# Gathering the preparation, row and routing pieces of a fused attention and expert kernel at one place per turn

## The chip, the cores and the metric

The kernel runs on one core of one Trainium2 chip. The metric is the device time of one execution in microseconds; the kernel before took 904.12 us (median of three runs, 903.97 to 904.96). The engines are called PE (TensorE, matmuls), PEld (its weight loads), DVE (VectorE), ACT (ScalarE), POOL (GpSimd) and SP (SyncE, which issues most DMAs). Each engine works through its own queue of instructions in order and waits on semaphores where it needs another engine's result.

## The reference

Two blocks follow each other. The first is a routed attention: for each of 4 batches and 8 heads, 768 queries and 768 keys of 64 values are each assigned to the nearest of 16 centroids, and a query attends only to keys of its own cluster. The second is a mixture of experts over the 3072 resulting rows of 512 values: a cosine router picks one of 8 experts for each row.

```python
q_assign = np.argmax(np.einsum('bhsd,hcd->bhsc', q_n, c_n), axis=-1)
k_assign = np.argmax(np.einsum('bhsd,hcd->bhsc', k_n, c_n), axis=-1)
mask = q_assign[:, :, :, None] == k_assign[:, :, None, :]
scores = np.where(mask, scale * np.matmul(q, k.transpose(0, 1, 3, 2)), -1e9)
attn = softmax(scores)                       # with 1e-9 added to the sum
x = rows of np.matmul(attn, v)               # (4*768, 8*64)
logits = xn @ en.T / tau                     # both rows normalized
expert_idx = np.argmax(logits, axis=1)
out[mask] = gate_w[mask, None] * (np.maximum(x[mask] @ w1[e], 0.0) @ w2[e])
```

## The kernel before

**Pairs, units and turns.** The attention works on pairs of heads: 16 pairs `n`, four for each batch. A pair has 12 units (two halves `hq` of the queries, six blocks `j` of 128 keys). For a unit, `scores` (L330) multiplies the block of keys with 384 queries of both heads into two PSUM banks, first with the one-hot cluster codes `kH`, `qH` (bf16) and then with `kT`, `qT` (fp32); `expo` (L346) takes the exponential on ACT into `prob`; `attend` (L351) multiplies `prob` with the values into `o_ps` and lets DVE add `prob` into `acc`. Six units make a group `g` (one half of the queries). After a group, `total` (L380) sums `acc` over the partitions on PE, ACT copies the sum as `den`, and `divide` (L395) takes a reciprocal on DVE and writes `xT`. Later `rows` (L412) transposes `xT` on PE, and ACT copies the rows into `xr`.

**Preparation of a pair.** `prep_pieces` (L209) returns ten pieces. `turn` transposes q or k, one half of the sequence at a time, three 128x128 transposes into one bank; ACT copies q, DVE copies k. `products` multiplies the transposed q and k with the centroids and ACT copies the result `asT`. `assign` transposes it back; DVE takes the maximum `amax` and compares (`sel`), POOL multiplies `sel` with a preference (L258). `choose` lets DVE take the maximum `pm` of that product and write the one-hot code `oh`. `turn_hot` transposes the code, six bf16 transposes into one bank for q (copied by DVE, L283) and for k (copied by ACT, L285). `values` adds up the values on POOL, and `mean` sums them on PE with a bank of its own (L298), from which DVE copies `ev`.

**Routing of a batch.** `route_pieces` (L429) returns five pieces: `products` of a half of the rows with the expert embeddings, `logits` with the squared norms of that half (three ACT instructions of 512 elements), the same for the other half, and `choose`, a chain of small operations on DVE, ACT (a square root and an exponential, each with its table) and POOL, which ends in a DMA of the rows to DRAM (`x_rows`).

**Banks.** All pieces, and `total`, take their PSUM bank from `misc()`: two banks in turn. `scores` has two buffers of two banks, `o_ps` two banks.

**Order.** The order on PE, DVE and ACT is that of the program (`manual_schedule`, L515); the order on SP and POOL is a planner's. The loop (L524) takes two units a turn, so a pair has six turns. One turn issues `scores` and `expo` of the two units after next, then one piece of preparation, then `rows` of the group before in the turns with `part == 4`, then `attend` of its two units, then `total` and `divide` where a group has just ended, then a second piece of preparation and one of routing. The pieces of pair `n+1` are worked through during pair `n`, one after the other, beginning with its first turn. `load` (L120) gets q, k and v of pair `n+1` at the beginning of pair `n`, through SP, each into two buffers; at pair 1 the first experts' weights follow.

After the last unit the loop runs on for three turns (`total`, `divide` and `rows` of the last group), and then come the five routing pieces of the last batch. After that a block of small operations finds each row's place (from L567), and the experts' stage (from L665) works through 28 blocks of 128 rows.

Of the kernel before, what the change touches and what calls it, by code (L numbers as in the profile page):

```python
# [9 lines left out]
F32 = mybir.dt.float32  # L10
BF16 = mybir.dt.bfloat16
I32 = mybir.dt.int32
ALU = mybir.AluOpType
ACTF = mybir.ActivationFunctionType
# [4 lines left out]
P = 128  # L19
# [16 lines left out]
def kernel(  # L36
# [12 lines left out]
    nc = tc.nc  # L49

    B, H, S, D = q.shape
# [4 lines left out]
    NJ = S // P  # L56
# [47 lines left out]
    with ExitStack() as at:  # L104
# [9 lines left out]
        def misc():  # L114
            return psM.tile([P, 512], F32, tag="misc", name="misc")
# [1 line left out]
        pairs = [(b, hp) for b in range(B) for hp in range(NHP)]  # L117
        ld = {}

        def load(n):  # L120
            b, hp = pairs[n]
            t = ld[n] = {}
            for nm, src in (("q", q), ("k", k), ("v", v)):
                t[nm] = ldp.tile([P, NJ, 2, D], F32, tag=nm + "32", name=nm + "32")
                for h in range(2):
                    nc.sync.dma_start(
                        out=t[nm][:, :, h],
                        in_=src[b, 2 * hp + h].rearrange("(p j) d -> p j d", j=NJ),
                    )

        c_sb = smp.tile([P, D], F32, name="c_sb", bufs=1)
        emb = smp.tile([E, DM], F32, name="emb", bufs=1)
        tau = smp.tile([E, 1], F32, name="tau", bufs=1)
        load(0)
        nc.scalar.dma_start(out=c_sb, in_=centroids.rearrange("h c d -> (h c) d"))
        nc.scalar.dma_start(out=emb, in_=moe_expert_emb)
        nc.scalar.dma_start(out=tau, in_=moe_tau.to_broadcast([E, 1]))
# [71 lines left out]
        def prep_pieces(n):  # L209
# [21 lines left out]
            def products():  # L231

                bk = misc()
                for i in range(4):
                    nc.tensor.matmul(  # L235
                        bk[2 * C * i : 2 * C * i + 2 * C, 0:HS],
                        lhsT=cnB[:, hp],
                        rhs=t["qk"[i // 2] + "T"][:, HS * (i % 2) : HS * (i % 2) + HS],
                        start=True,
                        stop=True,  # L240
                    )
                t["asT"] = smp.tile([P, HS], F32, tag="asT", name="asT")
                nc.scalar.copy(t["asT"], bk[:, 0:HS])

            def assign():
                bk = misc()
                for u in range(NJ // 2):
                    nc.tensor.transpose(  # L248
                        bk[:, P * u : P * u + P], t["asT"][:, P * u : P * u + P], ident
                    )  # L250
                shp = [P, 4 * NJ, C]
                asn = bk[:, 0 : 4 * NJ * C].rearrange("p (g c) -> p g c", c=C)
                amax = smp.tile(shp[0:2], F32, tag="amax", name="amax")
                sel = smp.tile(shp, BF16, tag="sel", name="sel")
                t["sel"] = sel
                nc.vector.tensor_reduce(amax, asn, axis=AXX, op=ALU.max)
                nc.vector.tensor_tensor(sel, asn, bc(amax, shp, 2), ALU.is_equal)  # L257
                nc.gpsimd.tensor_tensor(sel, sel, bc(prefc, shp, 1), ALU.mult)  # L258
# [12 lines left out]

            def turn_hot(i, nm):
                hot = t[nm + "H"] = trp.tile([P, S], BF16, tag=nm + "H", name=nm + "H")
                bk = misc().bitcast(BF16)
                for j in range(NJ):
                    half, u = divmod(j, NJ // 2)
                    nc.tensor.transpose(
                        bk[:, P * j : P * j + P],
                        oh[:, u, 2 * i + half].rearrange("p h c -> p (h c)"),
                        identb,  # L280
                    )
                if nm == "q":
                    nc.vector.tensor_scalar(hot, bk[:, 0:S], BIG, None, ALU.mult)  # L283
                else:
                    nc.scalar.copy(hot, bk[:, 0:S])  # L285

            def values():

# [4 lines left out]
                nc.gpsimd.tensor_tensor(vs[:, 0], vs[:, 0], vs[:, 2], ALU.add)  # L293
                t["vs"] = vs

            def mean():
                bk = misc()
                nc.tensor.matmul(  # L298
                    bk[:, 0:1],
                    lhsT=t["vs"][:, 0].rearrange("p h d -> p (h d)"),  # L300
                    rhs=epsc,
                    start=True,
                    stop=True,
                )
                t["ev"] = smp.tile([P, 1], F32, tag="ev", name="ev")
                nc.vector.tensor_copy(t["ev"], bk[:, 0:1])


            return [
                lambda: (turn("q", 0), turn("k", 0), values()),  # L310
                lambda: turn("q", 1),
                lambda: turn("k", 1),
                products,
                assign,
                choose,
                None,
                lambda: turn_hot(0, "q"),
                lambda: turn_hot(1, "k"),
                mean,
            ]  # L320


        GU = NJ
# [105 lines left out]
        def route_pieces(b):  # L429
# [4 lines left out]
            def products(half):  # L434

                if half == 0:
                    t["sq"] = smp.tile([P, NJ], F32, tag="sq", name="sq")
                    t["lg"] = smp.tile([P, NJ, E], F32, tag="lg", name="lg")
                bk = misc()
                for c in range(KD):  # L440
                    nc.tensor.matmul(  # L441
                        bk[2 * C * c : 2 * C * c + 2 * C, 0:HS],
                        lhsT=embT[:, c],
                        rhs=xT[b, half][:, c],
                        start=True,
                        stop=True,
                    )
                t["pT"] = smp.tile([P, HS], F32, tag="asT", name="asT")
                nc.scalar.copy(t["pT"], bk[:, 0:HS])

            def logits(half):
                bk = misc()
                for u in range(U):
                    nc.tensor.transpose(
                        bk[:, P * u : P * u + P], t["pT"][:, P * u : P * u + P], ident
                    )
                nc.vector.tensor_reduce(
                    t["lg"][:, U * half : U * half + U],
# [2 lines left out]
                    op=ALU.add,  # L461
                )

            def norms(half):
                for j in range(U * half, U * half + U):
                    junk = smp.tile([P, DM], F32, tag="junk", name="junk")
                    nc.scalar.activation(
                        junk, xr[b][:, j, 0:DM], ACTF.Square, accum_out=t["sq"][:, j : j + 1]
                    )

            def choose():
                lg, sq = t["lg"], t["sq"]
# [23 lines left out]
                    in_=xr[b],  # L496
                )

            return [
                lambda: products(0),  # L500
                lambda: (logits(0), norms(0)),
                lambda: products(1),
                lambda: (logits(1), norms(1)),
                choose,
            ]


        prepare, routing = [], []

        def prep():  # L510
            piece = prepare.pop(0) if prepare else None
            if piece:
                piece()

        with tc.manual_schedule(engines={EngineType.PE, EngineType.DVE, EngineType.Activation}):  # L515
            for piece in prep_pieces(0):
                if piece:
                    piece()
            for m in range(2):
                scores(m)  # L520
                expo(m)


            for i in range(0, len(units) + 6, 2):  # L524
                g, part = divmod(i, GU)
                if i < len(units) and i % (2 * NJ) == 0:
                    n = i // (2 * NJ)
                    assert not prepare
                    if n + 1 < len(pairs):
                        load(n + 1)  # L530
                        prepare = prep_pieces(n + 1)
                    if n == 1:

                        for w in range(2):
                            nc.sync.dma_start(
                                out=w1s[w], in_=moe_w1[0].rearrange("(c p) f -> p c f", p=P)
                            )
                            nc.sync.dma_start(
                                out=w2s[w], in_=moe_w2[0].rearrange("(c p) d -> p c d", p=P)
                            )  # L540
                for m in range(i + 2, min(i + 4, len(units))):
                    scores(m)
                    expo(m)
                prep()
                if part == 4 and g > 0:
                    rows(g - 1)
                for m in range(i, min(i + 2, len(units))):
                    attend(m)
                if part == 0 and g > 0:
                    total(g - 1)  # L550
                    divide(g - 1)
                prep()
                if routing:
                    routing.pop(0)()
                if part == 4 and g > 0 and g % (2 * NHP) == 0:
                    assert not routing
                    routing = route_pieces(g // (2 * NHP) - 1)
            for piece in routing:
                piece()


        with tc.tile_pool(name="rt", bufs=1) as rt:
# [247 lines left out]
```

## Time and profile before

| | |
|---|---|
| median of three runs | 904.12 us |
| the profiled execution, device time | 904.4 us |
| its span (first to last instruction) | 902.4 us |
| granted TensorE clock, mean | 0.973 |
| attention, first piece to pair 15 (25.61 to 423.97) | 398.36 us |
| last pair's rest, last routing and placing of rows (423.97 to 472.00) | 48.03 us, PE busy 26.24 |
| experts (472.00 to 902.4) | 430.40 us, PE busy 412.37 |

The profile page gives each engine's busy time and share of the span, the waits and the costliest groups of instructions. The timeline view lists instructions in order of time: start (us from the beginning of the span), duration, engine, source line, operation, what it writes and reads, how many of the same kind in a row, and in brackets the idle time of the engine just before and what ended it. The view by stretches gives, for parts of the span, the busy time of each engine with its number of instructions and the granted clock.

### The profile page before, as it was taken

How to read it: one execution, taken by the hardware profiler on the slowest of the kernel's cores; microseconds unless marked ns; L12 is line 12 of the kernel's file. 1: busy time of each engine (PE TensorE's matmuls, PEld its weight loads, DVE VectorE, ACT ScalarE, POOL GpSimd, SP SyncE). 2: the span in 40 equal slices, each digit the busy share in tenths (PEclk: the TensorE clock that was granted, in tenths of full speed). 3: DMA queues.
4: the chain of work that ended last, by engine and by line, in shares of the span. 5: the costliest groups of instructions: out<-in, count | busy, mean ns of one | idle time of the engine just before them, and what ended most of it. 6: DMA issues, size and time to landing. Idle time of an engine off the chain costs nothing.

```text
span 902.4 us, 12774 instructions
## 1 busy us (share of the span) xinstructions
PE 842.1 (93%) x5207; PEld 495.4 (55%) x5207; DVE 357.1 (40%) x488; ACT 301.6 (33%) x485; POOL 127.8 (14%) x171
## 2 busy tenths in 40 slices
PE   4999999999999999999628999999999999999996
PEld 2444444444444444444216777767676777767672
DVE  3577777877777877687750000000000000000000
ACT  3545556654566555755330111111111111111110
POOL 4011010211111111110021011110101010101010
PEclk8999999999999999999957999999999999999998
DMA  9822211322213122020011380756565656405610
GB/s 246 303 54 53 53 36 35 108 53 53 53 36 106 36 54 53 19 88 1 1 70 36 117 321 26 259 188 256 192 259 188 259 196 260 156 24 198 234 36 21
DMA packets 105645, 106.85 MB, mean 118 GB/s; under 512 B 77157, under 2 KB 77157, under 8 KB 105072
## 3 DMA queue, kind: packets, MB, share of 16 engines
q1 hardware_dynamic: 100928, 92.30, 31.8%
q0 software_dynamic: 4480, 13.65, 4.0%
q8 instruction: 43, 0.70, 0.3%
q14 instruction: 18, 0.15, 0.0%
q10 hardware_dynamic: 176, 0.05, 0.0%
HBM read 152.11 MB, written 13.64 MB: 184 GB/s over the span
## 4 chain that ended last, share of the span: by engine, by line
PE 38%; issue 28%; DMA 20%; DVE 9%; ACT 2%; POOL 1%; SPq 0%; POOLq 0%; DVEq 0%
DMA out_dram<-y,sidx 19%; PE s_ps L338 15%; PE o_ps L358 12%; DVE den L401 4%; PE misc L220 3%; PE misc L385 2%; PE misc L235 2%; PE misc L419 1%; DVE acc L377 1%; DVE xT L402 1%; ACT den L393 1%; PE misc L441 1%; PE misc L248 1%; DVE qH L283 1%; PE misc L298 1%
## 5 line engine op out<-in xcount | busy, mean ns | idle before, releaser
L714 PEld LDWEIGHTS h_ps<-xTm,w1s 128*128 128x128 f32 x1792 | 204.6, 193 | 22.1 <-DVE xTm L704 19.7
L714 PE MATMUL h_ps<-xTm,w1s 128*128 128x128 f32 x1792 | 208.7, 278 | 2.9 <-DMA w1s<-in_moe_w_dram 2.9
L727 PE MATMUL y_ps<-w2s,hT 128*128 128x512 f32 x448 | 201.2, 592 | 0.0
L349 ACT ACTIVATE prob<-s_ps 128x768 f32<-128x768 f32 x192 | 153.2, 811 | 100.2 <-PE s_ps L338 78.0
L704 DVE COPY xTm<-x_ps 128x512 f32<-128x512 f32 x28 | 19.4, 691 | 380.9 <-PE x_ps L702 380.9
L338 PE MATMUL s_ps<-qT,kT 64*128 64x384 f32 x768 | 156.3, 486 | 0.0
L358 PE MATMUL o_ps<-prob,v 128*64 128x384 f32 x768 | 145.1, 499 | 0.0
L377 DVE TENSOR_TENSOR acc<-acc,prob 128x768 f32<-128x768 f32 x128 | 130.1, 1017 | 4.9
L727 PEld LDWEIGHTS y_ps<-w2s,hT 128*128 128x128 f32 x448 | 81.0, 190 | 81.3 <-issue 81.3
L721 ACT ACTIVATE hT<-h_ps 128x512 f32<-128x512 f32 x56 | 33.4, 597 | 243.7 <-PE h_ps L714 243.7
L401 DVE RECIPROCAL den<-den 128x384 f32<-128x384 f32 x32 | 81.7, 2552 | 30.8 <-ACT den L393 30.8
L338 PEld LDWEIGHTS s_ps<-qT,kT 64*128 64x128 f32 x768 | 69.3, 190 | 21.3 <-issue 21.3
L736 POOL DMA_INDIRECT out_dram<-y,sidx x28 | 28.5, 1017 | 356.1 <-ACT y L735 350.2
L358 PEld LDWEIGHTS o_ps<-prob,v 128*64 128x64 f32 x768 | 46.5, 136 | 56.7 <-issue 55.1
L338 PE MATMUL s_ps<-qH,kH 64*128 64x384 bf16 x384 | 63.9, 329 | 1.6 <-ACT prob L349 1.3
L735 ACT ACTIVATE y<-y_ps,xin 128x512 f32<-128x512 f32 x28 | 19.2, 687 | 136.1 <-PE y_ps L727 129.9
L291 POOL TENSOR_TENSOR vs<-v 128x384 f32<-128x384 f32 x16 | 17.0, 1063 | 220.5 <-DMA v<-in_v_dram 220.5
L338 PEld LDWEIGHTS <-kH 64*128 64x128 bf16 x384 | 19.4, 94 | 51.7 <-issue 37.0
L229 DVE COPY kT<-misc 128x384 f32<-128x384 f32 x32 | 17.7, 553 | 54.0 <-PE misc L220 54.0
L258 POOL TENSOR_TENSOR sel<-sel,prefc 128x384 bf16<-128x384 bf16 x16 | 24.3, 1516 | 103.5 <-DVE sel L257 103.5
L393 ACT COPY den<-misc 128x384 f32<-128x384 f32 x32 | 15.3, 479 | 50.4 <-PE misc L385 50.4
L674 POOL DMA_INDIRECT xin<-x_rows,gidx x28 | 29.0, 1035 | 12.3 <-issue 8.2
(146 smaller groups left out, 511.8 us busy)
## 6 DMA issues: line engine op xcount, KB each, us to landing
w1s<-in_moe_w_dram SPq DMA_DIRECT2D x30, 2048.0 KB
w2s<-in_moe_w_dram SPq DMA_DIRECT2D x30, 2048.0 KB
x_rows<-xr SPq DMA_DIRECT2D x4, 1539.0 KB
q<-in_q_dram SPq DMA_DIRECT2D x32, 192.0 KB
k<-in_k_dram SPq DMA_DIRECT2D x32, 192.0 KB
v<-in_v_dram SPq DMA_DIRECT2D x32, 192.0 KB
xin<-x_rows,gidx POOLq DMA_INDIRECT x28, 7.2
out_dram<-y,sidx POOLq DMA_INDIRECT x28, 7.1
```

Source lines behind the costliest of these rows:

```text
L220: nc.tensor.transpose(bk[:, P * j : P * j + P], t[nm][:, NJ // 2 * half + j].rearrange("p h d -> p (h d)"), ident,)
L338: nc.tensor.matmul(s_ps[:, h, 0:HS], lhsT=t[l][rows, P * j : P * j + P], rhs=t[r][rows, HS * hq : HS * hq + HS], start=first, stop=not first,)
L349: nc.scalar.activation(d["prob"], d["s_ps"][:, :, 0:HS], ACTF.Exp)
L358: nc.tensor.matmul(g["o_ps"][D * h : D * h + D, 0:HS], lhsT=ld[n]["v"][:, j, h], rhs=d["prob"][:, h], start=(j == 0), stop=(j == NJ - 1),)
L377: nc.vector.tensor_tensor(g["acc"], g["acc"], d["prob"], ALU.add)
L393: nc.scalar.copy(d["den"], bk[:, 0:HS])
L401: nc.vector.reciprocal(d["den"], d["den"])
L674: nc.gpsimd.indirect_dma_start(out=xin, out_offset=None, in_=x_rows[:], in_offset=bass.IndirectOffsetOnAxis(ap=gidx[:, j : j + 1], axis=0) ...
L714: nc.tensor.matmul(bk[:, m : m + P], lhsT=w1s[j % 2][:, c, f0 + m : f0 + m + P], rhs=d["xT"][:, P * c : P * c + P], start=(c == 0), stop=( ...
L721: nc.scalar.activation(d["hT"][:, f0 : f0 + 512], bk, ACTF.Relu)
L727: nc.tensor.matmul(bk, lhsT=d["hT"][:, P * c : P * c + P], rhs=w2s[j % 2][:, c], start=(c == 0), stop=(c == KF - 1),)
L736: nc.gpsimd.indirect_dma_start(out=out[:], out_offset=bass.IndirectOffsetOnAxis(ap=sidx[:, j : j + 1], axis=0), in_=y, in_offset=None, bou ...
```

## The change

The pieces get names in place of an order of their own, and one function `between` says what is issued between `scores` and `attend` of each turn. Nothing is issued after `attend` any more but `total` and `divide` (and, in the very first turn, one piece). Each place holds pieces with two `misc` banks together: both transposes of a half of q and k; `products` and `rows`; `assign`, `choose` and `rows`; both `turn_hot`. `mean` has no bank of its own any more: it writes a spare column of the bank from which ACT copies `kH`, and is issued after that copy. The transposes of half 0 are done two pairs ahead, in the last turn of pair `n` for pair `n+2`, and q and k are loaded a pair earlier, v as before. Both `rows` of pair `n-1` stand in turns 1 and 2 of pair `n`. In routing, both `products` stand in turn 3 of the next batch's first pair, both `logits` and `choose` in turn 3 of its second pair, and the norms are issued one block a turn. At the end of the attention, the last batch's first half is routed before the last group is finished. `asT` and `sel` have one buffer each, and the routing has a buffer `pT` of its own.

```diff
-            def mean():
-                bk = misc()
+            def mean(bk):
+
+                col = slice(HS, HS + 1)
                 nc.tensor.matmul(
-                    bk[:, 0:1],
+                    bk[:, col],
                     lhsT=t["vs"][:, 0].rearrange("p h d -> p (h d)"),
...
             def turn_hot(i, nm):
                 hot = t[nm + "H"] = trp.tile([P, S], BF16, tag=nm + "H", name=nm + "H")
-                bk = misc().bitcast(BF16)
+                bank = misc()
+                bk = bank.bitcast(BF16)
...
                 else:
                     nc.scalar.copy(hot, bk[:, 0:S])
+                    mean(bank)
...
+            return {
+                "turn0": lambda: (turn("q", 0), turn("k", 0)),
+                "turn1": lambda: (turn("q", 1), turn("k", 1)),
+                "values": values,
+                "products": products,
+                "assign": lambda: (assign(), choose()),
+                "hots": lambda: (turn_hot(0, "q"), turn_hot(1, "k")),
+            }
...
+        def between(n, it):
+            b, nb = divmod(n, NHP)
+            if it == 5:
+                piece(n + 2, "turn0")
+                if n + 1 == NP:
+                    route[b] = route_pieces(b)
+                    rows(2 * n)
+                    route[b][0](0)
+            elif it == 0:
+                piece(n + 1, "turn1" if n else "turn0")
+            elif it == 1:
+                piece(n + 1, "values")
+                piece(n + 1, "products")
+                if n > 0:
+                    rows(2 * n - 2)
+            elif it == 2:
+                piece(n + 1, "assign")
+                if n > 0:
+                    rows(2 * n - 1)
+            elif it == 4:
+                piece(n + 1, "hots")
+            if b > 0:
+                if nb == 0 and it == 3:
+                    route[b - 1] = route_pieces(b - 1)
+                    for half in range(2):
+                        route[b - 1][0](half)
+                j = NJ * nb + it - 3
+                if 0 <= j < NJ:
+                    route[b - 1][2](j)
+                if nb == 1 and it == 3:
+                    for half in range(2):
+                        route[b - 1][1](half)
+                    route[b - 1][3]()
...
-            for i in range(0, len(units) + 6, 2):
-                g, part = divmod(i, GU)
...
+            load(1, "qk")
             for m in range(2):
                 scores(m)
                 expo(m)
+            for i in range(0, len(units), 2):
+                n, it = divmod(i // 2, NJ)
+                if it == 0 and n + 1 < NP:
+                    load(n + 1, "v")
+                if it == 4 and n + 2 < NP:
+                    load(n + 2, "qk")
...
                 for m in range(i + 2, min(i + 4, len(units))):
                     scores(m)
                     expo(m)
-                prep()
-                if part == 4 and g > 0:
-                    rows(g - 1)
-                for m in range(i, min(i + 2, len(units))):
+                between(n, it)
+                for m in range(i, i + 2):
                     attend(m)
-                if part == 0 and g > 0:
-                    total(g - 1)
-                    divide(g - 1)
-                prep()
-                if routing:
-                    routing.pop(0)()
...
+                if i % GU == 0 and i > 0:
+                    total(i // GU - 1)
+                    divide(i // GU - 1)
+                if i == 0:
+                    piece(1, "turn1")
+            total(ngroups - 1)
+            divide(ngroups - 1)
+            products, logits, norms, choose = route[B - 1]
+            for j in range(NJ // 2):
+                norms(j)
+            logits(0)
+            rows(ngroups - 1)
+            products(1)
+            for j in range(NJ // 2, NJ):
+                norms(j)
+            logits(1)
+            choose()
```

The new `piece(n, name)` issues one named piece of pair `n` if there is such a pair; `route_pieces` now returns its four functions `products`, `logits`, `norms` (of one block) and `choose`.

More of the change, by code (lines that the diff above doesn't have):

```diff
@@ L118, with load @@
         ld = {}
-        def load(n):
+        def load(n, names):
             b, hp = pairs[n]
-            t = ld[n] = {}
-            for nm, src in (("q", q), ("k", k), ("v", v)):
+            t = ld.setdefault(n, {})
+            for nm in names:
                 t[nm] = ldp.tile([P, NJ, 2, D], F32, tag=nm + "32", name=nm + "32")
@@ L127, in load @@
                         out=t[nm][:, :, h],
-                        in_=src[b, 2 * hp + h].rearrange("(p j) d -> p j d", j=NJ),
+                        in_={"q": q, "k": k, "v": v}[nm][b, 2 * hp + h].rearrange(
+                            "(p j) d -> p j d", j=NJ
+                        ),
                     )
@@ L133 @@
         tau = smp.tile([E, 1], F32, name="tau", bufs=1)
-        load(0)
+        load(0, "qkv")
         nc.scalar.dma_start(out=c_sb, in_=centroids.rearrange("h c d -> (h c) d"))
@@ L241, in products @@
                     )
-                t["asT"] = smp.tile([P, HS], F32, tag="asT", name="asT")
+                t["asT"] = smp.tile([P, HS], F32, tag="asT", name="asT", bufs=1)
                 nc.scalar.copy(t["asT"], bk[:, 0:HS])
@@ L253, in assign @@
                 amax = smp.tile(shp[0:2], F32, tag="amax", name="amax")
-                sel = smp.tile(shp, BF16, tag="sel", name="sel")
+                sel = smp.tile(shp, BF16, tag="sel", name="sel", bufs=1)
                 t["sel"] = sel
@@ L305, in mean @@
                 t["ev"] = smp.tile([P, 1], F32, tag="ev", name="ev")
[L306 to L320, printed above, removed]
+                nc.vector.tensor_copy(t["ev"], bk[:, col])
+            return {
[6 more added lines that the diff above has]
+            }
         GU = NJ
@@ L447, in products @@
                     )
-                t["pT"] = smp.tile([P, HS], F32, tag="asT", name="asT")
-                nc.scalar.copy(t["pT"], bk[:, 0:HS])
+                t["pT", half] = smp.tile([P, HS], F32, tag="pT", name="pT")
+                nc.scalar.copy(t["pT", half], bk[:, 0:HS])
             def logits(half):
@@ L454, in logits @@
                     nc.tensor.transpose(
-                        bk[:, P * u : P * u + P], t["pT"][:, P * u : P * u + P], ident
+                        bk[:, P * u : P * u + P], t["pT", half][:, P * u : P * u + P], ident
                     )
@@ L462, in logits, with norms @@
                 )
[L464 to L469, printed above, removed]
+            def norms(j):
+                junk = smp.tile([P, DM], F32, tag="junk", name="junk")
+                nc.scalar.activation(
+                    junk, xr[b][:, j, 0:DM], ACTF.Square, accum_out=t["sq"][:, j : j + 1]
+                )
             def choose():
@@ L497, in choose, with piece @@
                 )
[L499 to L513, printed above, removed]
+            return products, logits, norms, choose
+        NP = len(pairs)
+        prepare, route = {}, {}
+        def piece(n, name):
+            if n < NP:
+                if n not in prepare:
+                    prepare[n] = prep_pieces(n)
+                prepare[n][name]()
+        def between(n, it):
[31 more added lines that the diff above has]
+                    route[b - 1][3]()
         with tc.manual_schedule(engines={EngineType.PE, EngineType.DVE, EngineType.Activation}):
-            for piece in prep_pieces(0):
-                if piece:
-                    piece()
+            for name in ("turn0", "turn1", "values", "products", "assign", "hots"):
+                piece(0, name)
+            load(1, "qk")
             for m in range(2):
@@ L521 @@
                 expo(m)
-            for i in range(0, len(units) + 6, 2):
-                g, part = divmod(i, GU)
[L526 to L540, printed above, removed]
+            for i in range(0, len(units), 2):
[4 more added lines that the diff above has]
+                    load(n + 2, "qk")
+                if it == 0 and n == 1:
+                    for w in range(2):
+                        nc.sync.dma_start(
+                            out=w1s[w], in_=moe_w1[0].rearrange("(c p) f -> p c f", p=P)
+                        )
+                        nc.sync.dma_start(
+                            out=w2s[w], in_=moe_w2[0].rearrange("(c p) d -> p c d", p=P)
+                        )
                 for m in range(i + 2, min(i + 4, len(units))):
@@ L543 @@
                     expo(m)
-                prep()
-                if part == 4 and g > 0:
-                    rows(g - 1)
-                for m in range(i, min(i + 2, len(units))):
+                between(n, it)
+                for m in range(i, i + 2):
                     attend(m)
-                if part == 0 and g > 0:
-                    total(g - 1)
-                    divide(g - 1)
-                prep()
-                if routing:
-                    routing.pop(0)()
[L555 to L559, printed above, removed]
+                if i % GU == 0 and i > 0:
[15 more added lines that the diff above has]
+            choose()
         with tc.tile_pool(name="rt", bufs=1) as rt:
```

## The prediction

> **What bounds the kernel now.** I read the page first, then the busy time by stretch, then the timeline of one turn, then its end.
>
> ```profile
> span 902.4 us, 12774 instructions
> ...
> PE 842.1 (93%) x5207; PEld 495.4 (55%) x5207; DVE 357.1 (40%) x488; ACT 301.6 (33%) x485; POOL 127.8 (14%) x171
> ```
>
> ```profile
> 25.61:423.97 398.36, 389.93 (x2627) 179.73 (x2626) 299.82 (x371) 221.37 (x352) 54.77 (x75) 1.00 0.24 65
> ...
> 48.65:74.60 25.95, 25.54 (x174) 11.86 (x173) 19.67 (x22) 13.32 (x20) 3.46 (x4) 1.00 0.20 47
> ```
>
> The second view has one stretch per line: length, then busy time of PE, PEld, DVE, ACT, POOL, then the granted clock. Attention from the first preparation piece to pair 15 is TensorE throughout, at full clock; one pair takes 25.95 us, of which PE is busy 25.54. So only what lengthens or shortens PE's own queue counts. The expert stage (430 us) isn't touched. A pair has six steps, it 0 to 5, each `scores` of two units, then `attend` of two. From the starts of matmul groups in pair 1's timeline: scores 1.72, attend 1.44 (1.34 when `total` follows), total 0.75; six fp32 transposes together 0.80, three alone 0.48 (so a group of its own costs 0.16 above the 0.32 of three more); six bf16 transposes of `turn_hot` 0.44; `mean` 0.29.
>
> The same pair, its steps 2 to 4:
>
> ```profile
> 60.10 0.55 PE L248 MATMUL misc<-ident,asT 128*128 128x128 f32 x3
> ...
> 60.68 0.56 DVE L256 TENSOR_REDUCE amax<-misc 128x24 f32<-128x384 f32 x1 [1.26 <-PE misc L248]
> ...
> 61.27 0.56 DVE L257 TENSOR_TENSOR sel<-misc,amax 128x384 bf16<-128x384 f32 x1
> ...
> 61.75 2.53 DVE L377 TENSOR_TENSOR acc<-acc,prob 128x768 f32<-128x768 f32 x2
> 61.91 1.56 POOL L258 TENSOR_TENSOR sel<-sel,prefc 128x384 bf16<-128x384 bf16 x1 [6.91 <-DVE sel L257]
> ...
> 64.20 0.54 DVE L264 TENSOR_REDUCE pm<-sel 128x24 bf16<-128x384 bf16 x1
> ...
> 65.41 0.81 PE L385 MATMUL misc<-acc,ones 128*64 128x384 f32 x4
> ...
> 66.27 0.48 ACT L393 COPY den<-misc 128x384 f32<-128x384 f32 x1 [1.03 <-PE misc L385]
> ...
> 66.78 2.55 DVE L401 RECIPROCAL den<-den 128x384 f32<-128x384 f32 x1 [0.57 <-ACT den L393]
> ...
> 69.14 0.79 ACT L285 COPY kH<-misc 128x768 bf16<-128x768 bf16 x1
> ...
> 69.98 0.55 DVE L283 TENSOR_SCALAR qH<-misc 128x768 bf16<-128x768 bf16 x1
> ...
> 70.67 0.35 PE L298 MATMUL misc<-epsc,vs 128*128 128x1 f32 x2 [0.41 <-DVE qH L283]
> ```
>
> VectorE does the two `acc` adds while POOL multiplies `sel`, and takes `pm` after them; `total` (L385) doesn't wait. The one regular stall is `mean`: its bank is freed by the qH copy, so the attend before it takes 1.92 instead of 1.44.
>
> **The change, part by part.** Per steady pair:
>
> (a) The transposes of half 1 go together: 0.80 + 0.48 + 0.48 becomes 0.80 + 0.80: -0.16. (b) The two `turn_hot` go together: 0.44 + 0.44 less one group's 0.16, an estimate: -0.16 (bounds 0 and -0.16). (c) `products` runs one step after the transposes it reads; today its group takes 1.00 against 0.79 in pair 0, since the kT copy is behind the reciprocal on DVE: -0.21. It is now followed by `rows`, 0.78 + 0.48, as much as the two cost alone. (d) `mean`'s wait for the qH copy goes: -0.48.
>
> (e) `assign` and `choose` are now one piece, so on DVE amax, sel, pm, oh all stand ahead of the two adds of step 2, and pm waits for POOL. From the transposes' start: amax +0.58, sel +1.17 to +1.73, POOL from +1.81. How long POOL then takes: 1.56 beside the adds, 0.91 in pair 0's preparation, where DVE was idle; here DVE idles waiting for it, so I take 0.91, and keep 1.56 for the range.
>
> ```profile
> 15.82 0.91 POOL L258 TENSOR_TENSOR sel<-sel,prefc 128x384 bf16<-128x384 bf16 x1 [5.10 <-DVE sel L257]
> ```
>
> pm +2.76, oh until +3.9, two adds of 2.01 until +5.86, and total starts 0.14 after its last add where it waits for one (acc ends 444.56, total 444.70): +6.00. PE gets there at 0.80 (these transposes and rows') + 1.44 + 1.72 + 1.34 = +5.30. Stall +0.70. Queued behind on DVE are the next group's first add, the reciprocal and the qH copy; PE next asks for qH at the scores of step 5.
>
> (f) `mean` now writes a column of the bank that ACT reads for kH, and stands after that copy in the program. If the two are ordered, PE waits for ACT, whose queue has the step's two exps first: kH ends 3.34 after the step's scores begin (66.59 to 69.93), mean starts 0.06 later at +3.40; the hot transposes end at 1.72 + 0.72 = +2.44. Stall +0.97; queued behind it on PE is the whole attend of the step. No row shows a matmul writing beside a read of its bank. Bounds: 0 (no ordering) and 0.97; I take 0.97, as a shared bank is a dependency in every row there is (each group into `misc` follows the copy that empties it).
>
> The Trainium skill, "PSUM — Partial Sum Buffer", section "PSUM bank collisions raise a hardware error", says that a TensorE write and a ScalarE read of one bank at disjoint columns still collide and that software must guard by bank. No row here tests it; by that rule the wait is there and the sum is the one below, without it the sum is the first rival's.
>
> Sum per steady pair: -0.16 -0.16 -0.21 -0.48 +0.70 +0.97 = +0.66. After it, qH is ready about 5.2 after total starts (1.37 to the reciprocal, 4.6 to the copy, 0.55), and step 5's scores come at 0.75 + 3.69 + 1.44 = 5.88: no further stall.
>
> Routing. Today the two pairs that carry a batch's routing take 27.66 and 27.68, 3.4 above steady. Now: both `products` in step 3 add 0.69 + 0.78 to PE, of which 0.70 fills stall (e): +0.77. The norms go singly, one 0.82 pair of ACT instructions a step, under ACT's slack (13.3 busy of 25.95). Then `logits` and `choose` in step 3 of the next pair: the transposes (0.80) fill stall (e), +0.1, but choose's chain (two table loads of 1.28, about 14 DVE operations of 0.2) stands before the den copy, the reciprocal and qH. Followed through from step 3's start: adds done 3.62, lg 4.1, eq 5.2, sq and lg 6.05, ACT's Exp until 6.5, den 7.0, DVE's three operations until 7.2, first add 8.1, reciprocal 10.6, xT 11.3, qH 11.8; step 5's scores at 11.87 against 9.64 in a steady pair: +2.23. Per batch 3.0 against 3.4: -0.44, three times -1.3.
>
> Ends. Pair 0: three transposes' groups of 0.80 for 1.76 (+0.64), rows gone (-0.48), hots -0.16, mean -0.48 + 0.97, and with no rows to cover it the stall (e) is 1.02: +1.5. Pair 14 has no turn0 to do: +0.66 - 0.80 = -0.14. Pair 15 has rows(28): +0.48. Pair 0's preparation: mean now follows the kH copy instead of preceding the scores' wait for it: +0.3. Tail:
>
> ```profile
> 444.70 0.87 PE L385 MATMUL misc<-acc,ones 128*64 128x384 f32 x4 [2.09 <-DVE acc L377]
> ...
> 450.35 1.51 PE L441 MATMUL misc<-xT,embT 128*32 128x384 f32 x8
> ...
> 453.29 1.51 PE L441 MATMUL misc<-xT,embT 128*32 128x384 f32 x8
> ...
> 459.50 0.33 PE L568 MATMUL misc<-cumx,onesb 128*128 128x200 bf16 x1 [3.20 <-POOL cumx L484]
> ```
>
> Between the two L441 lie 2.94 us for half 0's products and logits, which now run earlier, as three norms do under the reciprocal; everything after moves up: -2.94. Their cover is the DVE adds and reciprocal before 449.4; without it they cost 2.94 again.
>
> Queues. On SP, q and k of pair n+2 already leave today as soon as their slot is free, a pair ahead (53.84 for 76.32), so needing them at step 5 of pair n costs nothing; v still waits for the last attend, and `values` on POOL starts 4 us behind it today too, in step 1. x_rows waits on SP for choose, some 7 us into step 3; a q and k load behind it would still have 6 us to land.
>
> 13 steady pairs x 0.66 = 8.6; -1.3; +1.5; -0.14; +0.48; +0.3; -2.94: **+6.5 us**. The profiled execution took 904.4, 0.3 above the median of 904.12: 910.9 against it, 910.6 as a median.
>
> **Rivals.**
> 1. *mean is not held by the kH copy.* Then qH gates step 5: scores there start at 5.2 after total instead of 5.88, 0.68 less in the twelve pairs where choose doesn't gate qH already (0 to 4, 6 to 8, 10 to 12, 14): -8.2, so -1.7: 902.4. For: the columns are disjoint. Against: program order and the shared bank.
> 2. *Both waits stay away* (the order on DVE is kept as today, pm and oh after the adds): -1.01 for each of 14 pairs, -1.3, -2.9, +0.8 for pair 15 and the start: 887. Against: the DVE order in the trace follows the program line by line, and the piece now is one.
> 3. *POOL needs 1.56 beside an idle DVE*: stall (e) is 1.35, +0.65 in 14 pairs: 919.7. Against: the 0.91 row.
>
> **How the numbers follow.** The forecast 0.66, rival 1 0.15, rival 2 0.07, rival 3 0.12. The predicted time is the forecast's, 910.6; its own range, with (b), (e) and (f) together off by 0.3 a pair, is 906 to 915. Rival 1 is taken in for the range, 902 to 915. Within 0.2% (what the measurement can tell from no change) is 902.3 to 905.9: half of rival 1, and a tenth of the forecast if the waits are half their size: 0.14. Faster 0.14: the other half and rival 2. Slower 0.72.
>
> **What would show it.** Right: total (L385) held some 0.7 us by `acc` in step 3 of every pair; mean (L298) held about 1 us by kH on ACT; POOL's sel at 0.91; DVE's pm idle before it and the adds behind oh; steady pairs of 26.6; total(31) to L568 shorter by 2.9. Wrong: pairs under 25.9, or an L298 that follows the transposes at once.

## The result, and the profile after

The changed kernel took 918.47 us (median of four runs, 917.95 to 919.82), the kernel before, beside it, 904.05 us: a ratio of 1.016, 95% interval 1.0142 to 1.0177. The change made the kernel slower by 1.6%. The forecast was 910.6 us, and the range 902 to 915 didn't hold the time.

The head of the page after the change, with the granted clock in 40 slices of 22.9 us:

```profile
span 917.9 us, 12757 instructions
...
PE 844.3 (92%) x5207; PEld 497.5 (54%) x5207; DVE 350.6 (38%) x488; ACT 303.0 (33%) x485; POOL 116.9 (13%) x171
...
PEclk8999999999998999989965999999999999999999
```

The span of the profiled executions grew by 15.5 us (the medians differ by 14.4), PE's busy time only by 2.2: PE waits more. The clock row has two dips in the attention (the 8s of the thirteenth and the eighteenth slice) which no term of the forecast accounts for.

By stretches (length, then busy time of PE, PEld, DVE, ACT and POOL, granted clock, DMA share and GB/s), the attention from its first piece to about its end, then pair 1:

```profile
27.03:442.25 415.22, 391.46 (x2624) 180.59 (x2622) 293.38 (x371) 222.39 (x351) 43.99 (x75) 0.98 0.23 61
...
51.69:78.46 26.77, 25.29 (x173) 11.69 (x173) 19.23 (x23) 13.46 (x20) 2.82 (x4) 1.00 0.21 45
```

Pair 1 takes 26.77 us instead of 25.95, with PE busy 0.25 us less: two new waits outweigh the work and the wait that were saved. They stand in the timeline of the same pair (start, duration, what it does, and in brackets the idle time of its engine before it):

```profile
62.44 0.55 PE L250 MATMUL misc<-ident,asT 128*128 128x128 f32 x3
...
63.62 0.56 DVE L259 TENSOR_TENSOR sel<-misc,amax 128x384 bf16<-128x384 f32 x1
...
64.26 0.91 POOL L260 TENSOR_TENSOR sel<-sel,prefc 128x384 bf16<-128x384 bf16 x1 [6.29 <-DVE sel L259]
...
65.20 0.55 DVE L266 TENSOR_REDUCE pm<-sel 128x24 bf16<-128x384 bf16 x1 [1.02 <-POOL sel L260]
...
66.26 2.01 DVE L377 TENSOR_TENSOR acc<-acc,prob 128x768 f32<-128x768 f32 x2
...
68.42 0.87 PE L385 MATMUL misc<-acc,ones 128*64 128x384 f32 x4 [0.50 <-DVE acc L377]
...
70.94 0.84 PE L280 MATMUL misc<-identb,oh 128*128 128x128 bf16 x12
...
71.82 0.80 ACT L288 COPY kH<-misc 128x768 bf16<-128x768 bf16 x1
...
72.77 0.35 PE L303 MATMUL misc<-epsc,vs 128*128 128x1 f32 x2 [0.98 <-ACT kH L288]
...
73.04 0.55 DVE L286 TENSOR_SCALAR qH<-misc 128x768 bf16<-128x768 bf16 x1
```

DVE idles 1.02 us for POOL's product, its two adds begin at 66.26, and `total` follows the last of them. The attend ahead of `total` thereby takes 2.01 instead of 1.34, a wait of 0.67, of which the view shows 0.50, as ends of matmuls are modelled. The twelve transposes of the codes are one group, and `mean` (L303) waits 0.98 us for ACT's copy of kH.

The end of the attention:

```profile
463.46 0.87 PE L385 MATMUL misc<-acc,ones 128*64 128x384 f32 x4 [1.30 <-DVE acc L377]
...
469.11 1.51 PE L441 MATMUL misc<-xT,embT 128*32 128x384 f32 x8
...
475.32 0.33 PE L599 MATMUL misc<-cumx,onesb 128*128 128x200 bf16 x1 [3.20 <-POOL cumx L483]
```

One L441 is left between the last total and L599, and that stretch is 11.86 us long instead of 14.80.

Pair 9 holds the `logits` and `choose` of a batch, in its step 3. What is behind `choose` on ACT, DVE and PE:

```profile
288.55 1.28 ACT L489 ACT_TABLE_LOAD   x1
...
289.92 1.09 PE L280 MATMUL misc<-identb,oh 128*128 128x128 bf16 x12
...
291.51 2.54 DVE L401 RECIPROCAL den<-den 128x384 f32<-128x384 f32 x1
...
292.39 0.79 ACT L288 COPY kH<-misc 128x768 bf16<-128x768 bf16 x1
...
293.33 0.56 PE L303 MATMUL misc<-epsc,vs 128*128 128x1 f32 x2 [2.32 <-ACT kH L288]
...
293.81 2.83 PE L358 MATMUL o_ps<-prob,v 128*64 128x384 f32 x8
...
296.57 0.50 PE L338 MATMUL s_ps<-qH,kH 64*128 64x384 bf16 x2
...
296.87 1.49 PE L338 MATMUL s_ps<-qT,kT 64*128 64x384 f32 x4
```

Here `mean` waits 2.32 us, and the next work is slow in itself: the eight matmuls of an attend take 2.83 us instead of 1.51, four of the scores 1.49 instead of 0.81. The same time by stretches:

```profile
289.35:292.76 3.41, 1.57 (x16) 0.73 (x14) 2.57 (x5) 2.88 (x6) 0.77 (x4) 1.00 0.41 173
292.76:296.18 3.42, 2.85 (x10) 1.27 (x10) 3.35 (x6) 0.42 (x1) 0.00 (x0) 0.50 0.69 288
296.18:299.59 3.41, 3.41 (x14) 1.45 (x12) 0.91 (x1) 0.81 (x1) 0.00 (x0) 0.50 0.00 0
299.59:303.00 3.41, 3.41 (x26) 1.76 (x26) 2.29 (x3) 1.19 (x2) 0.00 (x0) 1.00 0.00 0
```

In the stretch that ends at 292.76 PE is busy 1.57 of 3.41 us. Then the granted clock is 0.50 for two stretches of 3.41 us, and full again. Pair 5 has one such slow stretch (183.53 to 186.95), pair 13 two (405.40 to 412.23).

Where the 15.5 us came from, by the start of the scores in each pair's step 0 (us):

| part | forecast | measured |
|---|---|---|
| preparation of pair 0, and pair 0 | +1.8 | +3.04 |
| pairs 1–3, 6, 7, 10, 11 (25.95 to 26.77 each) | +4.6 | +5.8 |
| pairs 4, 8, 12, with both `products` of a batch | -0.8 | -0.5 |
| pairs 5, 9, 13, with `choose` (27.68 each to 30.08, 31.43, 31.52) | +3.8 | +10.0 |
| pair 14 | -0.14 | +0.02 |
| pair 15 | +0.48 | +0.48 |
| last total to L599 | -2.94 | -2.94 |
| experts | 0 | -0.3 |

The column of the forecast adds up to 6.8, not to its 6.5: the prediction took a batch's three terms, 0.77, 0.1 and 2.23, together as 3.0 instead of 3.1, which is 0.3 us for three batches.

### The profile page after: what moved, and what is told of

Its sections match the earlier page's. It is cut to its first block, busy times and chain, and to the rows that moved or that the text cites. A ratio compares the mean times of both kernels' runs of the same rounds, so it can differ in the third digit from the quotient of the medians.

```text
span 917.9 us, 12757 instructions
## 1 busy us (share of the span) xinstructions
PE 844.3 (92%) x5207; PEld 497.5 (54%) x5207; DVE 350.6 (38%) x488; ACT 303.0 (33%) x485; POOL 116.9 (13%) x171
## 4 chain that ended last, share of the span: by engine, by line
PE 38%; issue 28%; DMA 19%; DVE 7%; ACT 4%; POOL 2%; SPq 0%; POOLq 0%; DVEq 0%; ACTq 0%
DMA out_dram<-y,sidx 18%; PE s_ps L338 16%; PE o_ps L358 12%; PE misc L222 3%; PE misc L385 2%; DVE acc L377 2%; ACT prob L349 2%; ACT kH L288 1%; PE misc L237 1%; PE misc L419 1%; POOL sel L260 1%; PE misc L250 1%; PE misc L441 1%; PE misc L303 1%; DVE oh L267 1%
## 5 line engine op out<-in xcount | busy, mean ns | idle before, releaser
L338 PE MATMUL s_ps<-qT,kT 64*128 64x384 f32 x768 | 161.0, 499 | 0.0
L358 PE MATMUL o_ps<-prob,v 128*64 128x384 f32 x768 | 148.0, 507 | 0.0
L377 DVE TENSOR_TENSOR acc<-acc,prob 128x768 f32<-128x768 f32 x128 | 122.1, 954 | 3.7
L338 PEld LDWEIGHTS s_ps<-qT,kT 64*128 64x128 f32 x768 | 71.5, 196 | 23.2 <-issue 23.2
L385 PE MATMUL misc<-acc,ones 128*64 128x384 f32 x128 | 26.6, 492 | 6.1 <-DVE acc L377 6.1
L367 DVE SCALAR_TENSOR_TENSOR acc<-prob 128x768 f32<-128x768 f32 x32 | 30.3, 946 | 0.0
```

What stands on the lines that cost most here:

```text
L338: nc.tensor.matmul(s_ps[:, h, 0:HS], lhsT=t[l][rows, P * j : P * j + P], rhs=t[r][rows, HS * hq : HS * hq + HS], start=first, stop=not first,)
L358: nc.tensor.matmul(g["o_ps"][D * h : D * h + D, 0:HS], lhsT=ld[n]["v"][:, j, h], rhs=d["prob"][:, h], start=(j == 0), stop=(j == NJ - 1),)
L367: nc.vector.scalar_tensor_tensor(out=g["acc"], in0=un[i - 1]["prob"], scalar=NJ * EPS, in1=d["prob"], op0=ALU.add, op1=ALU.add,)
L377: nc.vector.tensor_tensor(g["acc"], g["acc"], d["prob"], ALU.add)
L385: nc.tensor.matmul(bk[D * h : D * h + D, 0:HS], lhsT=ones, rhs=d["acc"][:, h], start=True, stop=True,)
```

## The experiments

The theory after this reading: the two waits (e) and (f) are as forecast, and what was missed is the half clock after `choose`. Seven kernels, each the changed kernel with one edit unless said otherwise, tell the parts apart. Lines in their traces may stand a few numbers further on.

**The wait of `mean`.** `mean` writes into the bank of q's code, ahead of its copy by DVE, and no longer stands behind ACT's copy.

```diff
                 if nm == "q":
+                    mean(bank)
                     nc.vector.tensor_scalar(hot, bk[:, 0:S], BIG, None, ALU.mult)
+                    nc.vector.tensor_copy(t["ev"], bank[:, HS : HS + 1])
                 else:
                     nc.scalar.copy(hot, bk[:, 0:S])
-                    mean(bank)
```

> The changed kernel with one move: the mean matmul goes into the spare column of q's hot bank, ahead of the copy that reads it, and VectorE takes ev from there right after qH. Theory (mean is held by ScalarE's kH copy because it writes the bank which that copy reads): mean follows the twelve transposes at once, the attend of step 4 starts some 0.97 us sooner, and the next thing that holds PE is qH, ready 5.23 us after total starts, where PE is there at 5.09. A steady pair goes from 26.77 to 25.9; twelve pairs by 0.83, the pairs with the routing's choose keep their long wait (for qH now), and the first preparation gives back 0.5 to 1.5: 907 to 908 us. Rival (the bank is not what holds it, or the wait only moves on to another place of the same length): 916 us or more.

Measured: 903.78 us against 904.36 (ratio 0.9996, 0.9982 to 1.0009), span 900.8. Steady pairs take 25.92 us. PE in pair 2:

```profile
95.48 0.33 PE L304 MATMUL misc<-epsc,vs 128*128 128x1 f32 x2
...
97.83 0.34 PE L338 MATMUL s_ps<-qH,kH 64*128 64x384 bf16 x2 [0.22 <-DVE qH L287]
```

`mean` waits for nothing, and the scores of step 5 then wait 0.22 us for qH. That is the first rival's pair (25.95 + 0.66 - 0.68 = 25.93, with qH as the gate). The total came out some 4 us below the 907 to 908 expected: with `mean` free, PE's wait in the `choose` pairs moves to those scores (2.78 us in pair 5), and only one of three is followed by half clock. Pairs 5, 9, 13 take 28.61, 30.19, 28.60. The stretches around that wait in pairs 9 and 13:

```profile
283.56:286.97 3.41, 0.90 (x8) 0.66 (x10) 3.36 (x5) 0.47 (x1) 0.00 (x0) 1.00 0.71 296
286.97:290.39 3.42, 3.42 (x16) 1.94 (x14) 1.22 (x2) 2.08 (x3) 0.00 (x0) 0.50 0.00 0
...
392.79:396.20 3.41, 1.48 (x12) 0.88 (x12) 3.34 (x6) 0.46 (x1) 0.00 (x0) 1.00 0.57 242
```

The first, busy 0.90, is followed by half clock; the third, busy 1.48, isn't. In pair 5 the wait is cut by a boundary of the grid into stretches busy 0.55 and 0.64, and no drop follows.

**The wait of `total`.** `choose` of the clusters (`pm` and `oh` on DVE) is issued after the attend of step 2, behind the two adds, as before the change.

```diff
-                "assign": lambda: (assign(), choose()),
+                "assign": assign,
+                "choose": choose,
...
                 for m in range(i, i + 2):
                     attend(m)
+                if it == 2:
+                    piece(n + 1, "choose")
```

> The changed kernel with one move: the preparation's choose (pm and oh) stands behind the attend of step 2 again, so VectorE does the two adds while GpSimd multiplies. Theory (total waits for adds that stand behind the wait for GpSimd): total starts with no wait, GpSimd's multiply goes back from 0.91 to 1.56 us, and a steady pair loses 0.72 us; eight such pairs and 0.97 in pair 0, nothing in the pairs where routing work fills that gap: 911.8 us. Rival (total is late for another reason, such as the rows and products now beside it): 917 us or more.

Measured: 907.38 us (ratio 1.003, 1.0018 to 1.0041), span 905.9. Pair 1 in the timeline:

```profile
62.71 2.53 DVE L378 TENSOR_TENSOR acc<-acc,prob 128x768 f32<-128x768 f32 x2
...
62.87 1.56 POOL L260 TENSOR_TENSOR sel<-sel,prefc 128x384 bf16<-128x384 bf16 x1 [6.17 <-DVE sel L259]
...
66.36 0.81 PE L386 MATMUL misc<-acc,ones 128*64 128x384 f32 x4
```

The adds are beside POOL's product again (2.53 and 1.56 us, as before the change), and `total` doesn't wait. Steady pairs take 26.05, 0.72 less, which is (e)'s 0.67 and 0.05 of `total` itself. Pairs 4, 8 and 12 stay at 27.47: there the `products` of the routing cover the wait, as forecast. The total is 4.4 us lower than expected, chiefly by pairs 5, 9 and 13, to which the theory gave nothing and which took 5.1 us less (29.27, 29.33, 29.33). There are two reasons. What follows `total` comes sooner there too: `mean` starts 8.99 us after step 3 began, instead of 9.74. And these pairs have one slow stretch each instead of one, two and two.

**`choose` of the routing elsewhere.** It is moved from step 3 of the second pair to step 1 of the third, behind the attend.

```diff
                     for half in range(2):
                         route[b - 1][1](half)
-                    route[b - 1][3]()
...
+                if n // NHP > 0 and n % NHP == 2 and it == 1:
+                    route[n // NHP - 1][3]()
```

> The changed kernel with one move: the routing's choose goes from step 3 of a batch's second pair, ahead of attend, total and divide, to step 1 of its third pair, behind attend. Theory (choose stands before the den copy, the reciprocal and kH, PE then idles 2.3 us waiting at mean, and the granted clock falls to 0.50 for one or two stretches of 3.4 us afterwards): the second pairs fall from 30.1, 31.4 and 31.5 to 26.9, the third ones take some 1.3 us more, as choose costs in the kernel before, the clock stays at 1.00: 910 us. Rival (the half clock comes with the DMA of v or at a time of its own and not from the idle PE): the half-clock stretches stay, and only the schedule's own 2.2 us a batch less 1.3 come back: 915.7 us.

Measured: 910.66 us (ratio 1.0068, 1.0052 to 1.0085), span 910.8. The total is as expected, and so are the pairs, but for one. Pairs 5, 9, 13 come down to 26.85. Of the third pairs, 10 and 14 rise by 1.4 (26.77 to 28.17, 25.97 to 27.37), near the 1.3 expected; pair 6 rises by 3.0, to 29.80, since the clock did not stay at 1.00 there. In these pairs DVE's `amax` and what follows stand behind `choose`, so that the adds come late and `total` waits. Pair 6, PE's timeline and then its stretches:

```profile
204.01 0.87 PE L385 MATMUL misc<-acc,ones 128*64 128x384 f32 x4 [1.89 <-DVE acc L377]
```

```profile
202.03:205.44 3.41, 1.52 (x12) 0.69 (x12) 2.68 (x4) 1.29 (x2) 0.00 (x0) 1.00 0.43 178
205.44:208.86 3.42, 3.42 (x22) 1.86 (x16) 3.31 (x3) 1.62 (x2) 0.00 (x0) 0.50 0.00 0
```

A wait of 1.89 us, at another instruction and for another engine than in pair 9, is followed by half clock as well, while pairs 5, 9 and 13, whose loads of v stand where they stood, keep full clock. In pairs 10 and 14 the least busy stretches are at 0.52 and 0.53 of their length, and nothing follows.

**The wait filled with work.** In the three pairs of `choose`, twelve groups of three transposes, which write again what is there already, follow the transposes of k's code, ahead of its copy. The chain through DVE is untouched, and PE is busy during most of it.

```diff
+                    for _ in range(12 if n in (6, 10, 14) else 0):
+                        for u in range(NJ // 2):
+                            nc.tensor.transpose(
+                                bk[:, P * u : P * u + P],
+                                oh[:, u, 2 * i].rearrange("p h c -> p (h c)"),
+                                identb,
+                            )
```

> The changed kernel with work added and nothing taken away: in the three pairs with the routing's choose, 36 more bf16 transposes that write the same values again into k's hot bank, just ahead of the kH copy, so that PE is busy for about 2 us of the 2.3 us in which it waits at mean. Theory (the half clock follows from the idle PE): no stretch at 0.50 in these pairs, matmuls behind mean at full speed, 1.65 us back in the first of them and 2.9 in each of the other two: 911 us, faster although it does more. Rival (the clock falls for another reason): 918.5 us or more, with the same stretches at 0.50.

Measured: 911.63 us (ratio 1.0086, 1.0069 to 1.0103), span 909.0. Pair 9, its timeline on PE and ACT and the whole pair as a stretch:

```profile
289.73 2.17 PE L290 MATMUL misc<-identb,oh 128*128 128x128 bf16 x36
...
291.94 0.80 ACT L295 COPY kH<-misc 128x768 bf16<-128x768 bf16 x1 [0.56 <-PE misc L290]
...
292.88 0.35 PE L310 MATMUL misc<-epsc,vs 128*128 128x1 f32 x2 [0.98 <-ACT kH L295]
```

```profile
269.47:298.57 29.10, 28.04 (x215) 14.35 (x214) 21.58 (x37) 18.24 (x30) 4.01 (x10) 1.00 0.32 96
```

The clock stays at 1.00 through the pair, in all three, and each of them takes 29.10 us instead of 30.08, 31.43, 31.52. So it is the idle PE that the half clock follows, and not the DMA traffic of that time, which is the same: in the two stretches around `mean` the DMA engines are busy for 0.41 and 0.71 of the time here (288.24 to 295.07), and for 0.41 and 0.69 in the changed kernel.

With 36 matmuls more in each of three pairs the kernel is 6.8 us faster than the changed one. The three pairs give 5.73 us between the two profiled executions. The start gives only 0.14, as pair 0 is 0.89 shorter but begins 0.75 later; the rest of the attention gives nothing, and the experts' stage, the same in both kernels, happened to be 3.0 us shorter in this execution. The added transposes have a price of their own: ACT's copy of kH waits 0.56 us for them, and `mean` starts 10.41 us after step 3 began, instead of 9.74.

**The product on DVE.** DVE does POOL's product itself; its order is otherwise the changed kernel's.

```diff
-                nc.gpsimd.tensor_tensor(sel, sel, bc(prefc, shp, 1), ALU.mult)
+                nc.vector.tensor_tensor(sel, sel, bc(prefc, shp, 1), ALU.mult)
```

> The changed kernel with the product of sel done by VectorE in place of GpSimd, and the order unchanged: pm and oh still stand ahead of the two adds, but wait for nobody. Theory (total is late by the whole chain amax, sel, GpSimd, pm, oh ahead of the adds): GpSimd's 0.91 and its two hand-overs of 0.04 and 0.08 become one VectorE operation of some 0.57, so total's wait of 0.67 shrinks to about 0.2 and does not go: 914.3 us. Rival (only the wait for GpSimd counts): as without the wait, 912 us or less. Rival (GpSimd has no part in it): 918.5 us.

Measured: 907.68 us (ratio 1.0039, 1.0024 to 1.0053), span 908.1. Pair 1:

```profile
62.72 0.36 DVE L260 TENSOR_TENSOR sel<-sel,prefc 128x384 bf16<-128x384 bf16 x1
...
64.17 2.01 DVE L377 TENSOR_TENSOR acc<-acc,prob 128x768 f32<-128x768 f32 x2
...
66.34 0.87 PE L385 MATMUL misc<-acc,ones 128*64 128x384 f32 x4
```

The product takes 0.36 us where 0.57 had been assumed, `total` is held 0.08 instead of 0.67, and a steady pair takes 26.18 instead of 26.77. So the way to POOL and back (0.91 us and the handovers) is enough to account for nearly all of (e). So are `pm` and `oh`, some 1.1 us together, which the second experiment took from ahead of the adds: the chain overruns what PE has to do meanwhile by 0.67 us, and shortening it at either place is enough. Most of what the total fell beyond the expected 914.3 is again in pairs 5, 9, 13 (29.48, 29.49 and 29.48, one slow stretch each); here too what follows `total` comes sooner (`mean` at 9.15 us instead of 9.74).

**Both waits away.** The first two edits together.

> The two moves of the first two experiments together: mean in q's hot bank ahead of its copy, and the preparation's choose behind the attend of step 2. Theory (two separate waits on PE, at total and at mean, and behind both the qH copy, which is ready 5.23 us after total starts): neither total nor mean waits; a steady pair takes 16.05 to total, 5.3 from there to step 5's scores, 3.97 for step 5: 25.3 us, so the gains add up but for some 0.2 that qH takes back. The long wait in the pairs with the routing's choose stays, now at step 5's scores. 894 us. Rival (the two waits are one and the same delay seen in two places, so the second move brings nothing): 903 us.

Measured: 896.76 us against 904.46 (ratio 0.9909, 0.9893 to 0.9926), span 895.8; faster than before by 0.9%. Steady pairs take 25.20, the pairs of `choose` 29.44, 29.49, 27.86, the first two with a slow stretch. The savings of the two edits add up: 26.77 less 0.85 less 0.72 is 25.20.

**And `choose` at step 4.** As the last one, and the routing's `choose` is issued after the attend of step 4 of the same pair: behind the qH copy on DVE and the kH copy on ACT, so that nothing PE asks for soon is behind it.

```diff
-                    route[b - 1][3]()
...
+                if n // NHP > 0 and n % NHP == 1 and it == 4:
+                    route[n // NHP - 1][3]()
```

> The same two moves and the routing's choose behind the attend of step 4 in the batch's second pair, in place of step 3 ahead of attend, total and divide. Theory: choose no longer stands before den, the reciprocal, kH and qH; ScalarE's two table loads then delay the exps of step 5, and PE waits 0.6 to 1.3 us once a batch; no stretch at half clock in the pairs. Second pairs at 26 to 26.6, steady ones at 25.3: 888 us, faster than both kernels. Rival (choose costs the same wherever it stands, as in the kernel before, where it takes 1.3 us, plus the half clock): 892 us or more.

Measured: 889.22 us (ratio 0.9828, 0.9811 to 0.9844), span 888.6: the fastest of all, 1.7% below the kernel before. Pair 1 and pair 5 as stretches:

```profile
50.08:75.28 25.20, 24.97 (x173) 11.75 (x172) 19.66 (x23) 13.40 (x20) 3.47 (x4) 1.00 0.22 48
...
152.33:178.87 26.54, 25.85 (x180) 12.49 (x179) 20.79 (x36) 17.18 (x29) 4.65 (x10) 1.00 0.21 47
```

A steady pair leaves PE 0.23 us idle, and one with `choose` takes 26.54, 1.14 less than before the change, at full clock.

## Why the prediction was wrong in size

**What held.** The sign, and the mechanism: PE's own queue is what counts, it got shorter, and two new waits in every pair outweighed that. Of the steps per pair, (a) the grouped transposes, (c) `products` without its wait and (d) the old wait of `mean` came out as worked out. Stall (e) at `total` was 0.67 for 0.70, and stall (f) at `mean` 0.98 for 0.97. The last agreement is partly luck: `mean` came 3.54 us after the step's scores, not 3.40, and the transposes before it were 0.13 longer than assumed. POOL took 0.91 us beside an idle DVE, so rival 3 fell. Rival 1, that `mean` isn't held by ACT's copy, fell too; the run that takes the hold away gave its pair time, and so agrees with its arithmetic (25.92 for 25.93). Rival 2, that both waits stay away, isn't what this change did; the run without both took 896.76 us against the 887 worked out for it, and half of that miss is in the pairs of `choose`, which took 29.44, 29.49 and 27.86 instead of some 27.3 (24.94, a steady pair's in that rival, and 2.33). The Trainium skill, "PSUM — Partial Sum Buffer", section "PSUM bank collisions raise a hardware error", asks for a guard by bank even where the columns differ; the wait for kH is there in this trace, 0.98 us, though it shows only that the two are ordered, not what an unordered access would do. The end, pair 15 and the cover of the first `products` by (e) held to 0.3 us.

**What failed: the routing's "+2.23".** The order of events behind that term was right: in pair 5, qH was done 11.58 us after step 3 began (11.8 forecast), and the scores of step 5 came at 11.82 (11.87). But the step priced idle time as idle time alone, at full clock. `choose` left PE with nothing to do for 2.3 us, in front of `mean`, and what follows such a gap ran at half clock for 3.41 or 6.83 us. So these pairs took 3.31, 4.66 and 4.75 us more than a steady pair, where the forecast had 2.33 (2.23 for `choose` and 0.1 for the transposes of the logits). That is 5.73 of the 9.0 us by which the span missed the sum.

At full clock the term of 2.33 would have been too large, not too small. With `mean` moved, pair 5 has qH at the same 11.58, no slow stretch, and takes 28.61 us: 1.84 above the changed kernel's steady pair. So the half clock itself cost some 7.2 us, an estimate from 30.08, 31.43 and 31.52 less 28.61 each. And that a pair with the wait filled took 29.10, which is 26.77 and just the forecast's 2.33, is a coincidence: about 0.5 of it is the price of the added transposes.

**The smaller misses.** Step (b), the grouping of the code's transposes, was put at -0.16 a pair and is worth -0.03: twelve together take 0.85 us, two sixes took 0.88. A `total` that had to wait takes 0.80 rather than 0.75. These two make a steady pair 0.82 dearer instead of 0.66, and with 13 of them are 2 us. About 1.1 us more is at the start of pair 0, where the clock came up to full at 26.5 us instead of 23.5. In the experiments whose records show it, that time lay between 24.1 us (`mean` moved) and 26.9 (the fastest kernel); whether the change shifts it isn't shown, as it was not tried by itself.

**What the experiments' own misses say.** Three totals (`mean` moved, `choose` of the clusters split off, the product on DVE) came out some 4, 4.4 and 6.6 us lower than expected. The steady pair moved as it should, but for the product's own price, 0.21 us off. What differed most is the number of slow stretches, one, three and three against five, since each edit shifts or shortens the waits against the 3.41 us grid; and in the last two, what follows `total` in the pairs of `choose` came 0.75 and 0.59 us sooner, which the expectations left out. Such totals can't be added up to a microsecond. Nor does one profile stand for all executions: with `mean` moved, five of ten took 901.8 to 902.8 us at a mean granted clock of 0.974 to 0.978, and five took 904.8 to 907.0 at 0.967 to 0.971. The one that was profiled, with its single slow stretch, is of the first five; where the others lost their clock isn't shown.

## What to carry to other kernels

In a loop that PE bounds, an instruction on another engine, or one of PE that waits for a copy, should be issued where PE does not soon ask for what is queued behind it: the grouping saved PE work here, but in the kernels tried it paid off (25.20 us a pair against 25.95) only when `pm` and `oh` stood behind the adds again and `mean` no longer behind the kH copy. A side chain like the routing's `choose` belongs right after the last result that the main engine needs soon (26.54 us a pair, against 27.86 to 29.49 for the same kernel with `choose` ahead of it). And where the profile shows a wait of some 2 us on PE, look at the granted clock behind it before pricing it; here filling it with repeated work was cheaper than leaving it (29.10 us a pair against 30.08 to 31.52).

## What was not expected of the hardware

The half clock came after gaps of PE that are shorter than its own step. By the records of six executions (the changed kernel and the five of the experiments that had a drop), cut on the 3.41 us grid on which the clock changed, thirteen stretches with PE busy between 0.26 and 0.47 of the time were followed by half clock; one at 0.43 wasn't (pair 13 with `mean` moved); none at 0.52 or more was. The regular wait of 0.98 us in each pair leaves its stretch at 0.71 and never did harm. The Trainium skill, "TensorE: Matmul & The Clock Gate", section "Why this matters for your kernels", warns of gaps on PE over about 3 us; here a gap of 1.82 us was enough (at `mean` in pair 5 with the clusters' `choose` split off; PE busy 1.59 of 3.41), so a stretch less than half busy describes these runs better, with the one exception. Why pairs 9 and 13 had two slow stretches in a row and pair 5 one stays open: in the former PE was busy 2.85 and 3.03 us of the first of them, in the latter all of it. The other ten drops of these records lasted one stretch each, with PE busy all of it. That would fit a clock which comes back once a whole stretch was busy, but nothing was run to test it.

The same product of 384 bf16 elements a partition took 0.91 us on POOL with DVE idle, 1.56 beside DVE's adds, which themselves went from 2.01 to 2.53 for two, and 0.36 on DVE.
